# Scores of the next pair placed behind the output and state sums, with those sums in ring banks

## The chip, the cores and the metric

The kernel runs on one core of a Trainium2 chip. The metric is the device time of one execution in microseconds (us), the median of several runs. A profile of one execution gives a span (first to last instruction) that is a few us shorter than that time. The engines are called as in the profile: PE is TensorE (PEld its weight loads), DVE is VectorE, ACT is ScalarE, POOL is GpSimd, SP is SyncE, which only issues transfers here.

## What is computed

The reference is a state-space layer in chunks (4 batches, 8 heads, 768 positions, head dimension 32, state dimension 16) followed by a bilinear feed-forward over all 3072 tokens:

```python
for c in range(nc):                                   # chunks of 32 in the reference
    cum = np.cumsum(la, axis=-1)
    L = np.exp(cum[..., :, None] - cum[..., None, :]) * causal
    M = np.einsum('bhin,bhjn->bhij', Cc, Bc) * L      # "scores", masked
    y = M @ xc + (Cc @ state) * np.exp(cum)           # within the chunk, and from the state
    state = decay_full * state + sum_j(Bc x xc * decay_from_j)
x = y.transpose(0, 2, 1, 3).reshape(3072, 256)
out = ((x @ w_a) * (x @ w_b)) @ w_out                 # 256 -> 1536 -> 256
```

The result does not depend on the length of the chunks; the kernel takes 128.

## The kernel before, in words

**Pairs.** The work is cut into 12 pairs p: two batches of the four (index bt within a pair) times one block of 128 positions. Pairs 0 and 1 are block 0, pairs 2 and 3 block 1, and so on. A pair's state comes from pair p-2. The decay factors are folded into B and C when they are scaled, so that the scores need only a 0/1 mask.

**What is done for one pair.**

- `load` brings B, C and x in; `scale` multiplies them on POOL (`bm`, `cm`, `x16`; lines 231 and 237).
- `transposes` turns `bm` and `cm` on PE into the bank TT, which is a part of the tile SC0 (line 255); ACT copies them out three times (`bt` twice at line 262, `ct` at line 263).
- `scores` makes 32 small matmuls (tiles of 32 rows by 64 columns) into the four banks SC0 and SC1 (line 276). `mask(product(p, m))` multiplies one of the four banks by the causal mask into `t1` on DVE (line 309), in the prologue sometimes on POOL by way of ACT (lines 306 and 307).
- `pv` makes the output: four inter-chunk matmuls from the state (`sbd`, line 352; not for block 0), 32 small ones for the sums within the block (line 318), and 16 small ones for the state sums (`ds_mm`, line 335). Then ACT copies the output into `X2T` (line 364). In the kernel before, all of this lies in the two banks of SC1.
- `state` updates the state on DVE (lines 386 and 388), and POOL spreads it into `sbd` (line 392) and scales it for later (`gU`, line 399).
- `unit(p, k2)`, six for each pair, is one sixth of the feed-forward's first layer: four matmuls with w_a into `aps`, four with w_b into `bps` (line 417), a copy of `aps` to `asb` on ACT (line 426) and the product of `bps` and `asb` into `hk` on DVE (line 427). `go` makes whole units one after the other.
- `out_half(p, bt)` is the second layer for one batch: 12 matmuls into `ops` (line 434), a copy on ACT (line 449), a store.

**Banks.** `psf` is a pool of four accumulation banks with one tag. `aps`, `bps`, `ops` (and in the changed kernel `py0`, `py1`) each take one of them. A bank can be written again when the last reader of its old tile is done. The other four banks are SC0 and SC1.

**Order.** The schedule is manual: each engine gets its instructions in the order in which the program writes them, and semaphores are put where one engine needs another. After a prologue for pairs 0 to 2 the loop from p = 3 interleaves the scores of pair p, the six units of pair p-1, the two output halves of pair p-2, the output and state sums of pair p and the transposes of pair p+1:

```python
    for p in range(3, NP):
        scores(p)
        ...
        h = unit(p - 1, 0)
        mask(product(p, 0))
        h()
        ...
        out_half(p - 2, 0)
        go((p - 1, 3))
        pull(p); pv(p); state(p)
        transposes(p + 1)
        out_half(p - 2, 1)
        go((p - 1, 4), (p - 1, 5))
```

(shortened; the masks 1 to 3, unit 1 and unit 2 lie where the dots are.) After the loop come the units of pair 11 with the halves of pair 10 between them, and then the halves of pair 11.

Of the kernel before, what the change touches and what calls it, by code (L numbers as in the profile page):

```python
# [22 lines left out]
def kernel(  # L23
# [103 lines left out]
    def load(p, eng=None):  # L127
        tiles(p)
        return [load1(eng or nc.sync, p, w, bt) for w in range(3) for bt in range(2)]
# [115 lines left out]
    def scale(p):  # L245
        scale_bc(p, 1, nc.gpsimd)
        scale_bc(p, 0, nc.gpsimd)
        scale_x(p, nc.gpsimd)

    def transposes(p, ps=None):  # L250
        s = st[p]
        TB, TC = (TT[:, 0:256], TT[:, 256:512]) if ps is None else [t_.bitcast(f16)[:, 0:256] for t_ in ps]
        for T_, src in ((TB, s["bm"]), (TC, s["cm"])):
            for r in range(2):
                nc.tensor.transpose(  # L255
                    T_[:, r * 128 : (r + 1) * 128], src[:, r].rearrange("p h n -> p (h n)"), ident
                )
        BT = mid.tile([128, 2, 2, 2, 64], f16, name="bt", tag="bt")
        CT = mid.tile([128, 2, Q], f16, name="ct", tag="ct")
        for e in range(2):  # L260
            o_ = BT[:, e].rearrange("p r t i -> p (r t i)")
            nc.scalar.activation(out=o_, in_=TB, func=AF.Copy, scale=par[:, e : e + 1])  # L262
        (nc.scalar.copy if ps is None else nc.vector.tensor_copy)(
            CT.rearrange("p t (i r) -> p r (t i)", r=2), TC.rearrange("p (r c) -> p r c", r=2)
        )
        s["BT"], s["CT"] = BT, CT

    def scores(p):
        BT, CT = st[p]["BT"], st[p]["CT"]
        for e in range(2):  # L270
            for r in range(2):
                for m in range(4):
                    for bt in range(2):
                        rows = slice(32 * m, 32 * m + 32)
                        c0 = (e * 2 + r) * Q
                        nc.tensor.matmul(  # L276
                            SC[m][64 * bt : 64 * bt + 64, c0 : c0 + Q],
                            BT[rows, e, r, bt],
                            CT[rows, bt],
                            start=True,  # L280
                            stop=True,
                            skip_group_check=True,
                            tile_position=(32 * m, 64 * bt),
                        )
        st[p]["T1"] = mid.tile([128, H, 2, Q], f16, name="t1", tag="t1")

    def product(p, m):

        return (
            st[p]["T1"][:, 2 * m : 2 * m + 2].rearrange("p e r q -> p e (r q)"),  # L290
            SC[m].rearrange("p (e c) -> p e c", e=2),
        )
# [18 lines left out]
    def pv_u(p, u, py, first):  # L311
        s = st[p]
        for r in range(2):
            for g in range(4):
                for bt in range(2):
                    h = u * 4 + g
                    k = slice(64 * bt, 64 * bt + 64)
                    nc.tensor.matmul(  # L318
                        py[bt][32 * g : 32 * g + 32, u * Q : (u + 1) * Q],
                        s["X16"][k, h, r, :],  # L320
                        s["T1"][k, h, r, :],
                        start=(first and u == 0 and r == 0),
                        stop=(r == 1),
                        skip_group_check=True,
                        tile_position=(64 * bt, 32 * g),
                    )

    def ds_mm(p, c0):
        s = st[p]
        s["DS"] = [SC1[:, bt, c0 : c0 + 2 * D] for bt in range(2)]  # L330
        for r in range(2):
            for m in range(4):
                for bt in range(2):
                    k = slice(64 * bt, 64 * bt + 64)
                    nc.tensor.matmul(  # L335
                        s["DS"][bt][32 * m : 32 * m + 32, :],
                        s["bm"][k, r, 2 * m : 2 * m + 2, :].rearrange("p h n -> p (h n)"),
                        s["X16"][k, 2 * m : 2 * m + 2, r, :],
                        start=(r == 0),
                        stop=(r == 1),  # L340
                        skip_group_check=True,
                        tile_position=(64 * bt, 32 * m),
                    )

    def pv(p):
        blk, bp = divmod(p, NBP)
        s = st[p]
        PY = [SC1[:, bt, 0:256] for bt in range(2)]
        if blk > 0:
            for bt in range(2):  # L350
                for u in range(2):
                    nc.tensor.matmul(  # L352
                        PY[bt][:, u * Q : (u + 1) * Q],
                        s["Sbd"][:, bt, u * 128 : u * 128 + 128],
                        s["CT"][:, bt],
                        start=(u == 0),
                        stop=False,
                        skip_group_check=True,
                    )
        for u in range(2):  # L360
            pv_u(p, u, PY, blk == 0)
        if blk < NBLK - 1:
            ds_mm(p, 256)
        nc.scalar.activation(  # L364
            out=X2T[:, p].rearrange("p u t q -> p t u q"),
            in_=SC1[:, :, 0:256].rearrange("p t (u q) -> p t u q", u=2),
            func=AF.Copy,
            scale=YS / XS,
        )

    def evac0(u, bt, eng, py):
        o_, i_ = X2T[:, 0, u, bt], py[bt][:, u * Q : (u + 1) * Q]
# [34 lines left out]
    def unit(p, k2):  # L407
        s = st[p]
        if k2 == 0:
            s["hk"] = ffh.tile([128, NK, 2 * Q], f16, name="hk", tag="hk")  # L410
        a_ps = psf.tile([128, 512], f32, name="aps", tag="ff")
        b_ps = psf.tile([128, 512], f32, name="bps", tag="ff")
        for ps, W in ((a_ps, Wa), (b_ps, Wb)):
            for kk in range(2):
                k = 2 * k2 + kk
                for f in range(2):
                    nc.tensor.matmul(  # L417
                        ps[:, kk * 2 * Q : (kk + 1) * 2 * Q],
                        W[:, f, k * 128 : (k + 1) * 128],
                        X2T[:, p, f].rearrange("p t q -> p (t q)"),  # L420
                        start=(f == 0),
                        stop=(f == 1),
                        skip_group_check=True,
                    )
        asb = ffh.tile([128, 512], f32, name="asb", tag="asb")
        nc.scalar.copy(asb, a_ps)  # L426
        return lambda: nc.vector.tensor_tensor(  # L427
            out=s["hk"][:, 2 * k2 : 2 * k2 + 2, :].rearrange("p k q -> p (k q)"), in0=b_ps, in1=asb, op=ALU.mult
        )
# [23 lines left out]
    def out_half(p, bt):  # L453
        o_ps = psf.tile([128, 512], f32, name="ops", tag="ff")
        out_mm(p, bt, o_ps, range(NK))
        out_store(p, bt, o_ps)


    def bank(name):
        return psf.tile([128, 512], f32, name=name, tag="ff")  # L460

    def fb(k):
        nc.vector.reciprocal(flat(fB, k, k + 1), flat(fC, k, k + 1))  # L463

    def go(*items):
        for p, k2 in items:
            unit(p, k2)()

    def pull(p):
        if ("S", p) in st:  # L470
            st[p].update(st.pop(("S", p)))
# [68 lines left out]
    nc.scalar.copy(G.rearrange("p b g -> p (b g)"), gps[:, 0 : nb * NG])  # L540
    fb(1)
    scale(2)
    pv(1)
    ds_mm(0, 320)
    state(0)
    state(1)
    go((1, 0), (1, 1))
# [11 lines left out]
    h = unit(1, 4)  # L559
    mask(product(2, 1))  # L560
    h()
    go((1, 5))
    pull(2)
    pv(2)
    state(2)
    fb(2)
    load(4)
    transposes(3)
    out_half(0, 0)
    out_half(0, 1)  # L570

    for p in range(3, NP):
        scores(p)
        if p + 1 < NP:
            scale(p + 1)
        if p + 2 < NP:
            load(p + 2)
        h = unit(p - 1, 0)
        mask(product(p, 0))
        h()  # L580
        mask(product(p, 1))
        mask(product(p, 2))
        h = unit(p - 1, 1)
        h()
        mask(product(p, 3))
        go((p - 1, 2))
        out_half(p - 2, 0)
        go((p - 1, 3))
        pull(p)
        pv(p)  # L590
        state(p)
        if p + 1 < NP:
            transposes(p + 1)
        out_half(p - 2, 1)
        if p % 2 == 0 and p // 2 + 1 < NBLK:
            fb(p // 2 + 1)
        go((p - 1, 4), (p - 1, 5))

    go((NP - 1, 0), (NP - 1, 1))
    out_half(NP - 2, 0)  # L600
    go((NP - 1, 2), (NP - 1, 3))
    out_half(NP - 2, 1)
    go((NP - 1, 4), (NP - 1, 5))
    o = [psf.tile([128, 512], f32, name="ops", tag="ff") for _ in range(2)]
    for bt in range(2):
        out_mm(NP - 1, bt, o[bt], range(NK - 2))
# [33 lines left out]
```

## Time and profile before

| what | value | from |
|---|---|---|
| time, median of 3 runs | 137.73 us (137.08 to 137.8) | times |
| span of the profiled execution | 134.0 us | page |
| DVE line 427 (`hk`) | 72 x 687 ns | page, groups |
| ACT line 426 (`asb`) | 72 x 587 ns | page, groups |
| DVE line 309 (mask) | 44 x 681 ns | page, groups |
| ACT line 262 (`bt`) | 22 x 472 ns | page, groups |
| ACT line 449 (copy of an output half) | 23 x 385 ns | page, groups |
| POOL line 392 (`sbd`) | 10 x 1159 ns, 36.0 us idle before it | page, groups |
| ACT line 426 waits for PE's `aps` | 18.4 us, 45 times | waits |

How to read it: the page gives, for each engine, the busy time and its share of the span; below that the span in 40 equal slices with a digit for the busy tenths and one for the clock that PE was granted. A row of the groups names the line, the engine, the operation, the tiles written and read with their shapes, and the count; behind the bar stand the busy time, the mean duration of one, the idle time of the engine ahead of it and what ended that idle time. A row of the timeline has the start in us, the duration in us, the engine, the line, the operation, the tiles and the count; in brackets the idle time ahead of it and who ended it. Ends of matmuls are modelled, and neighbouring matmuls overlap in the record, so distances between starts are the better measure on PE.

### The profile page before, as it was taken

To read this page: it belongs to the slowest core of one execution; us is meant where nothing else is said; L and a number is where in the kernel's file an instruction comes from. 1 tells how busy PE (TensorE), PEld (TensorE's weight loads), DVE (VectorE), ACT (ScalarE), POOL (GpSimd) and SP (SyncE) were. 2 spreads that over 40 slices of the span, in tenths; PEclk is the share of its full clock that TensorE was granted. 3 is DMA by queue.
4 is the path that set the end of the run, shared out by engine and by line. 5 is a ranking of instruction groups with operands and counts; after the bars stand their busy time and mean duration, and the time that the engine had idled before them with its cause. 6 is when DMAs were issued, how large, how long until landed. Compare 5 with 4: busy or idle time off the path is not lost.

```text
span 134.0 us, 4722 instructions
## 1 busy us (share of the span) xinstructions
PE 125.1 (93%) x1946; PEld 102.8 (77%) x1946; DVE 86.2 (64%) x162; ACT 75.1 (56%) x154; POOL 55.5 (41%) x74
## 2 busy tenths in 40 slices
PE   6985798998999999999999999999999999999990
PEld 2332675887888888889888888888888888888870
DVE  1676138678277595793994974975947929834440
ACT  3162454696457647657548556576476576455420
POOL 6941906699940922904706608409128000000000
PEclk9999756999999999999999999999999999999999
DMA  3999999955146262451551451623611011110112
GB/s 72 169 179 195 159 188 178 183 102 112 42 86 151 72 117 64 91 109 39 108 134 39 64 137 54 111 80 72 126 47 39 5 50 33 39 39 5 41 37 78
DMA packets 44805, 12.22 MB, mean 91 GB/s; under 512 B 38576, under 2 KB 44752, under 8 KB 44784
## 3 DMA queue, kind: packets, MB, share of 16 engines
q1 hardware_dynamic: 38784, 9.04, 32.1%
q0 software_dynamic: 3216, 2.36, 12.2%
q10 hardware_dynamic: 2784, 0.52, 2.3%
q8 instruction: 15, 0.25, 0.8%
q14 instruction: 6, 0.05, 0.1%
HBM read 11.13 MB, written 3.15 MB: 107 GB/s over the span
## 4 chain that ended last, share of the span: by engine, by line
PE 73%; DMA 9%; SPq 8%; POOL 6%; issue 1%; DVE 0%; POOLq 0%
PE ops L434 24%; PE aps L417 20%; PE bps L417 20%; DMA xn<-in_x_dram 9%; SPq L122 8%; PE SC L276 2%; PE SC L318 2%; PE SC L255 2%; POOL sbd L392 2%; PE SC L352 1%; POOL t L307 1%; POOL x L231 1%; PE SC L335 1%; POOL gU L399 1%; POOL bm L237 0%
## 5 line engine op out<-in xcount | busy, mean ns | idle before, releaser
L427 DVE TENSOR_TENSOR hk<-bps,asb 128x512 f16<-128x512 f32 x72 | 49.3, 687 | 28.7 <-ACT asb L426 24.6
L426 ACT COPY asb<-aps 128x512 f32<-128x512 f32 x72 | 42.1, 587 | 20.0 <-PE aps L417 18.4
L417 PE MATMUL aps<-X2T,Wa 128*128 128x256 f16 x288 | 44.3, 277 | 0.0
L417 PE MATMUL bps<-X2T,Wb 128*128 128x256 f16 x288 | 44.2, 277 | 0.0
L434 PE MATMUL ops<-Wo,hk 128*128 128x256 f16 x288 | 35.0, 273 | 0.0
L417 PEld LDWEIGHTS <-Wb 128*128 128x128 f16 x288 | 28.5, 99 | 4.1 <-issue 0.2
L309 DVE TENSOR_TENSOR t<-SC,causal 128x512 f16<-128x512 f32 x44 | 29.0, 681 | 3.7 <-ACT osb L449 2.4
L417 PEld LDWEIGHTS <-Wa 128*128 128x128 f16 x288 | 27.4, 99 | 4.7 <-DVE X2T L376 0.3
L434 PEld LDWEIGHTS <-hk 128*128 128x128 f16 x288 | 27.7, 98 | 3.2
L392 POOL TENSOR_TENSOR sbd<-U,maskbd 128x512 f16<-128x512 f32 x10 | 11.6, 1159 | 36.1 <-DVE U L388 36.0
L449 ACT ACTIVATE osb<-ops 128x256 f32<-128x256 f32 x23 | 8.9, 385 | 17.0 <-PE ops L434 16.9
L231 POOL TENSOR_SCALAR x<-xn 128x512 f16<-128x512 f32 x10 | 14.9, 1492 | 1.9 <-DMA xn<-in_x_dram 1.1
L262 ACT ACTIVATE bt<-SC,ch 128x256 f16<-128x256 f16 x22 | 9.2, 472 | 2.7 <-PE SC L255 2.5
L364 ACT ACTIVATE X2T<-SC 128x512 f16<-128x512 f32 x11 | 6.6, 597 | 6.5 <-PE SC L335 4.8
L237 POOL TENSOR_TENSOR cm<-cn,fC 128x256 f16<-128x256 f32 x11 | 6.8, 621 | 3.1 <-DMA cn<-in_C_dram 3.1
L237 POOL TENSOR_TENSOR bm<-bn,fB 128x256 f16<-128x256 f32 x11 | 6.8, 622 | 0.9 <-DVE fB L463 0.9
L388 DVE SCALAR_TENSOR_TENSOR U<-SC,G,gU 128x64 f32<-128x64 f32 x16 | 3.8, 280 | 4.7 <-ACT X2T L364 4.7
L307 POOL TENSOR_TENSOR t<-tmp,causal 128x512 f16<-128x512 f32 x4 | 4.6, 1154 | 5.0 <-ACT tmp L306 5.0
L185 PE MATMUL SC<-warm 128*128 128x512 f16 x10 | 4.8, 628 | 1.2 <-DVE warm L149 1.2
L276 PE MATMUL SC<-ct,bt 32*64 32x128 f16 x384 | 5.9, 234 | 0.1
L276 PEld LDWEIGHTS <-bt 32*64 32x64 f16 x384 | 3.9, 109 | 2.7 <-issue 1.9
L255 PE MATMUL SC<-ident,bm 128*128 128x128 f16 x22 | 3.1, 224 | 2.6 <-POOL bm L237 2.6
(59 smaller groups left out, 73.2 us busy)
## 6 DMA issues: line engine op xcount, KB each, us to landing
xn<-in_x_dram SPq DMA_DIRECT2D x23, 128.0 KB, 3.1
out_dram<-osb SPq DMA_DIRECT2D x23, 128.0 KB, 1.7
bn<-in_B_dram SPq DMA_DIRECT2D x24, 64.0 KB, 2.7
cn<-in_C_dram SPq DMA_DIRECT2D x20, 64.0 KB, 3.1
Wa<-in_moe_w_a_dram POOLq DMA_DIRECT2D x3, 256.0 KB, 5.6
Wb<-in_moe_w_b_dram POOLq DMA_DIRECT2D x3, 256.0 KB, 6.5
Wo<-in_moe_w_out_dram POOLq DMA_DIRECT2D x1, 768.0 KB, 10.8
cn<-in_C_dram ACTq DMA_DIRECT2D x4, 64.0 KB, 4.6
```

The costliest lines, as they stand in the source:

```text
L122: return eng.dma_start(pair_in[p][which][64 * bt : 64 * bt + 64].rearrange("i h r n -> i h (r n)"), src.rearrange("h (i r) n -> i h (r n)" ...
L231: eng.tensor_scalar(xo, xi, XS, None, ALU.mult)
L237: eng.tensor_tensor(out=m_, in0=pair_in[p][which].rearrange("p h r n -> p r h n"), in1=f[:, blk, :, bp].unsqueeze(3).broadcast_to((128, 2, ...
L262: nc.scalar.activation(out=o_, in_=TB, func=AF.Copy, scale=par[:, e : e + 1])
L276: nc.tensor.matmul(SC[m][64 * bt : 64 * bt + 64, c0 : c0 + Q], BT[rows, e, r, bt], CT[rows, bt], start=True, stop=True, skip_group_check=True,
L309: nc.vector.tensor_tensor(out=o_, in0=i_, in1=c_, op=ALU.mult)
L392: nc.gpsimd.tensor_tensor(out=Sbd.rearrange("p t (m c) -> p t m c", m=4), in0=U32[:, p].unsqueeze(2).broadcast_to((128, 2, 4, 2 * D)), in1 ...
L417: nc.tensor.matmul(ps[:, kk * 2 * Q : (kk + 1) * 2 * Q], W[:, f, k * 128 : (k + 1) * 128], X2T[:, p, f].rearrange("p t q -> p (t q)"), sta ...
L426: nc.scalar.copy(asb, a_ps)
L427: return lambda: nc.vector.tensor_tensor(out=s["hk"][:, 2 * k2 : 2 * k2 + 2, :].rearrange("p k q -> p (k q)"), in0=b_ps, in1=asb, op=ALU.mult)
L434: nc.tensor.matmul(o_ps[:, 0:d_model], hk[:, k, bt * Q : (bt + 1) * Q], Wo[:, k, :], start=(k == 0), stop=(k == NK - 1), skip_group_check= ...
L449: nc.scalar.activation(out=o_sb, in_=o_ps[:, 0:d_model], func=AF.Copy, scale=1.0 / (YS * YS))
```

## The change

The tiled matmuls of the scores (32 x 64 tiles) and those of the output and state sums (64 x 32 tiles) stood at two places of a loop turn, with full-size feed-forward matmuls between them. The change puts the scores of pair p+1 directly behind the output and state sums of pair p, so that the small tiled matmuls come in one stretch. For this the output and state sums can no longer lie in SC1, which the scores write; they go into two banks of the ring (`py0`, `py1`). The rest of the turn follows from that: both output halves of pair p-1 come next, then the six units of the same pair p, with the transposes of pair p+2 between units 3 and 4. Scaling and loading run one pair further ahead. The masks of pair p+1 are issued in one go behind the first output half. The copy into `X2T` becomes one for each batch. In the prologue `transposes(3)` moves ahead of unit (1, 5), scores(3) behind `pv(2)`, and the halves of pair 1 come directly behind those of pair 0.

```diff
-    def ds_mm(p, c0):
+    def ds_mm(p, py, c0):
         s = st[p]
-        s["DS"] = [SC1[:, bt, c0 : c0 + 2 * D] for bt in range(2)]
+        s["DS"] = [py[bt][:, c0 : c0 + 2 * D] for bt in range(2)]
...
     def pv(p):
-        blk, bp = divmod(p, NBP)
-        s = st[p]
-        PY = [SC1[:, bt, 0:256] for bt in range(2)]
+        blk = p // NBP
+        py = [bank("py0"), bank("py1")]
         if blk > 0:
...
+            inter(p, py)
         for u in range(2):
-            pv_u(p, u, PY, blk == 0)
+            pv_u(p, u, py, blk == 0)
         if blk < NBLK - 1:
-            ds_mm(p, 256)
-        nc.scalar.activation(
-            out=X2T[:, p].rearrange("p u t q -> p t u q"),
-            in_=SC1[:, :, 0:256].rearrange("p t (u q) -> p t u q", u=2),
-            func=AF.Copy,
-            scale=YS / XS,
-        )
+            ds_mm(p, py, 256)
+        return py
+
+    def evac(p, py):
+        for bt in range(2):
+            nc.scalar.activation(
+                out=X2T[:, p, :, bt],
+                in_=py[bt][:, 0:256].rearrange("p (u q) -> p u q", u=2),
+                func=AF.Copy,
+                scale=YS / XS,
+            )
...
-    pv(1)
-    ds_mm(0, 320)
+    py = pv(1)
+    ds_mm(0, py, 320)
+    evac(1, py)
...
     h()
+    transposes(3)
     go((1, 5))
     pull(2)
-    pv(2)
+    py = pv(2)
+    scores(3)
+    evac(2, py)
     state(2)
     fb(2)
     load(4)
-    transposes(3)
     out_half(0, 0)
+    mask(product(3, 0))
     out_half(0, 1)
+    mask(product(3, 1))
+    scale(4)
+    load(5)
+    out_half(1, 0)
+    mask(product(3, 2))
+    out_half(1, 1)
+    mask(product(3, 3))
+    go((2, 0), (2, 1), (2, 2), (2, 3))
+    transposes(4)
+    go((2, 4), (2, 5))
 
     for p in range(3, NP):
...
+        pull(p)
+        py = pv(p)
         if p + 1 < NP:
-            scale(p + 1)
+            scores(p + 1)
+        evac(p, py)
+        state(p)
         if p + 2 < NP:
...
+            scale(p + 2)
+        if p + 3 < NP:
+            load(p + 3)
+        out_half(p - 1, 0)
         if p + 1 < NP:
...
+            for m in range(4):
+                mask(product(p + 1, m))
+        out_half(p - 1, 1)
+        go((p, 0), (p, 1))
+        if p % 2 == 1 and (p + 3) // 2 < NBLK:
+            fb((p + 3) // 2)
+        go((p, 2), (p, 3))
+        if p + 2 < NP:
+            transposes(p + 2)
+        go((p, 4), (p, 5))
```

More of the change, by code (lines that the diff above doesn't have):

```diff
@@ L343, in ds_mm, with inter @@
                     )
+    def inter(p, py):
+        s = st[p]
+        for bt in range(2):
+            for u in range(2):
+                nc.tensor.matmul(
+                    py[bt][:, u * Q : (u + 1) * Q],
+                    s["Sbd"][:, bt, u * 128 : u * 128 + 128],
+                    s["CT"][:, bt],
+                    start=(u == 0),
+                    stop=False,
+                    skip_group_check=True,
+                )
     def pv(p):
-        blk, bp = divmod(p, NBP)
-        s = st[p]
-        PY = [SC1[:, bt, 0:256] for bt in range(2)]
+        blk = p // NBP
+        py = [bank("py0"), bank("py1")]
         if blk > 0:
[L350 to L358, printed above, removed]
-                    )
+            inter(p, py)
         for u in range(2):
-            pv_u(p, u, PY, blk == 0)
+            pv_u(p, u, py, blk == 0)
         if blk < NBLK - 1:
-            ds_mm(p, 256)
-        nc.scalar.activation(
-            out=X2T[:, p].rearrange("p u t q -> p t u q"),
-            in_=SC1[:, :, 0:256].rearrange("p t (u q) -> p t u q", u=2),
-            func=AF.Copy,
-            scale=YS / XS,
-        )
+            ds_mm(p, py, 256)
+        return py
+    def evac(p, py):
+        for bt in range(2):
+            nc.scalar.activation(
[3 more added lines that the diff above has]
+                scale=YS / XS,
+            )
     def evac0(u, bt, eng, py):
@@ L567 @@
     load(4)
-    transposes(3)
     out_half(0, 0)
+    mask(product(3, 0))
     out_half(0, 1)
+    mask(product(3, 1))
[8 more added lines that the diff above has]
+    go((2, 4), (2, 5))
     for p in range(3, NP):
-        scores(p)
+        pull(p)
+        py = pv(p)
         if p + 1 < NP:
-            scale(p + 1)
+            scores(p + 1)
+        evac(p, py)
+        state(p)
         if p + 2 < NP:
[L577 to L591, printed above, removed]
-        if p + 1 < NP:
[L593 to L603, printed above, removed]
+            scale(p + 2)
+        if p + 3 < NP:
+            load(p + 3)
+        out_half(p - 1, 0)
+        if p + 1 < NP:
+            for m in range(4):
[8 more added lines that the diff above has]
+        go((p, 4), (p, 5))
     o = [psf.tile([128, 512], f32, name="ops", tag="ff") for _ in range(2)]
```

## The prediction

> **What bounds the kernel now.** I read the page's busy table and slices first, to see which engine could set the end; then the stages of the loop; then the timeline of TensorE over one pair; then the timelines of ScalarE and GpSimd at two places of the prologue.
>
> ```profile
> PE 125.1 (93%) x1946; PEld 102.8 (77%) x1946; DVE 86.2 (64%) x162; ACT 75.1 (56%) x154; POOL 55.5 (41%) x74
> ...
> PEclk9999756999999999999999999999999999999999
> ```
>
> TensorE is busy in 93% of the span and the granted clock is full but for three slices before 24 us. A busy share is an average, so the stages come next (columns: stretch, length, PE busy and count, clock, DMA share, GB/s):
>
> ```profile
> 54.65:64.03 9.38, 9.38 (x162) 1.00 0.40 86
> 64.03:73.42 9.39, 9.39 (x164) 1.00 0.40 86
> 73.42:82.80 9.38, 9.38 (x163) 1.00 0.40 87
> ```
>
> Each stretch is one turn of the main loop (from the scores of one pair to those of the next). It has no gap on TensorE. So a turn gets shorter only by TensorE work that goes away, and every wait that the change puts in front of TensorE is paid in full. The turn in start order (start, duration):
>
> ```profile
> 54.12 0.60 PE L417 MATMUL bps<-X2T,Wb 128*128 128x256 f16 x4
> 54.65 0.43 PE L276 MATMUL SC<-ct,bt 32*64 32x128 f16 x32
> 55.01 0.61 PE L417 MATMUL aps<-X2T,Wa 128*128 128x256 f16 x4
> 55.45 0.60 PE L417 MATMUL bps<-X2T,Wb 128*128 128x256 f16 x4
> ...
> 59.82 0.39 PE L352 MATMUL SC<-ct,sbd 128*128 128x128 f16 x4
> 60.14 0.42 PE L318 MATMUL SC<-t,x 64*32 64x128 f16 x32
> 60.39 0.32 PE L335 MATMUL SC<-x,bm 64*32 64x64 f16 x16
> 60.65 0.28 PE L255 MATMUL SC<-ident,bm 128*128 128x128 f16 x2
> 60.77 0.28 PE L255 MATMUL SC<-ident,cm 128*128 128x128 f16 x2
> 60.88 1.47 PE L434 MATMUL ops<-Wo,hk 128*128 128x256 f16 x12
> ```
>
> I use distances between starts, since a matmul's end is modelled. A group of four feed-forward matmuls takes 0.44 us (55.01 to 55.45), a unit of two groups 0.875, one output half 1.31 (60.88 to the next group at 62.19). Four 128-column matmuls take 0.23 in the transposes (60.65 to 60.88), but 0.32 where the tiled output sums follow (59.82 to 60.14), and a group takes 0.53 where the tiled scores follow (54.12 to 54.65). So **going between full and tiled matmuls costs about 0.1 us**. A turn is 6 units 5.25 + 2 halves 2.62 + 0.45 for the scores (0.09 before, 0.36 with the way back) + 1.06 for inter-chunk, output sums, state sums and transposes (59.82 to 60.88) = 9.38.
>
> **The Trainium skill.** "TensorEngine Tiling (Array Packing)", Key Properties, says that a change of tiling mode drains TensorE; the 0.09 to 0.1 us above agree. "PSUM — Partial Sum Buffer", Engine vs sequencer instructions, says that matmuls start and complete in program order; so one that waits for a bank holds all behind it, and the timeline shows no exception. "Perfetto Trace Analysis", Optimization Strategy, says that the same gap repeating on the engine that should be saturated can mean that there is too little SBUF or PSUM for the next tile. Before has no such gap in the loop; I expect after to get one.
>
> **Part 1: scores moved behind the state sums.** No matmul is added or removed. A turn before changes between full and tiled four times: into and out of the scores, and around the output and state sums. After, the tiled groups stand together: in, from state sums to scores (both tiled, other shapes), and out. If the change between two tiled shapes also costs 0.1, a turn saves one change, 0.1; if it is free, 0.2; if 16 small state sums run badly into the scores, 0. I take 0.1, keep 0 and 0.2. It acts on about 7 turns after the prologue: **-0.7 us** (0 to -1.4).
>
> **Part 2: the output sums move into the ring of four banks (psf).** Before, they lay in SC1, which nothing else needed then. Now py0 and py1 take two ring banks directly behind units 4 and 5. Which banks, the built program tells by its waits: py0 waits for ScalarE's copy of unit 4's aps, py1 for its copy of unit 5's aps (a bank is handed on in order of release). What ScalarE does just then: the transposes of pair p+2 now stand before units 4 and 5, so three copies of transposes (bt, bt, ct) stand in its queue ahead of those two copies. Before had 1.31 us of an output half between transposes and units. The prologue of before has exactly the new sequence once (transposes of pair 2, two units, then other work):
>
> ```profile
> 25.29 0.59 ACT L426 COPY asb<-aps 128x512 f32<-128x512 f32 x1 [0.29 <-PE aps L417]
> 25.89 0.84 ACT L262 ACTIVATE bt<-SC,ch 128x256 f16<-128x256 f16 x2
> 26.62 0.45 ACT L263 COPY ct<-SC 128x256 f16<-128x256 f16 x1
> 26.92 1.08 ACT L426 COPY asb<-aps 128x512 f32<-128x512 f32 x2
> ```
>
> There the transposes start at 25.47 and the last group of the second unit at 27.00, so TensorE is free at 27.44. The two copies end at about 27.5 and 28.00. Put py0 and py1 there: py0's two matmuls start at about 27.5 and take 0.11; py1 could start at 27.55 but waits for 28.00 and the way of the semaphore. For that way the trace gives 0.04 (L364 ends 23.48, ds_mm(0) starts 23.52) to 0.2. So **TensorE stands 0.5 us in every turn** (0.45 to 0.65). Behind the waiting py1 matmul stand output sums, state sums, next scores and both halves, so nothing fills it. A floor for the case that ScalarE is faster than I think: without transposes, aps 5 starts 0.875 before TensorE is free, the copy starts 0.69 after that (52.81 to 53.50), takes 0.59, ends at +0.40, and py1 would start at +0.11: still 0.35 with the semaphore. The turns into pairs 3 to 10 have transposes (8 x 0.5 = 4.0), the one into pair 11 has none (0.35). Sum **+4.35** (3.1 to 5.6). The py banks of pair 2 come free before the wait of Part 3, and cost nothing.
>
> **Part 3: the prologue.** transposes(3) moves ahead of unit (1,5) and pv(2). It needs bm of pair 3 from GpSimd:
>
> ```profile
> 29.25 2.28 POOL L307 TENSOR_TENSOR t<-tmp,causal 128x512 f16<-128x512 f32 x2
> 31.48 0.62 POOL L237 TENSOR_TENSOR cm<-cn,fC 128x256 f16<-128x256 f32 x1
> 32.06 0.62 POOL L237 TENSOR_TENSOR bm<-bn,fB 128x256 f16<-128x256 f32 x1
> ```
>
> GpSimd works without a gap from 24.71, when x of pair 2 lands, to 32.68, and its order up to there stays. TensorE before fills that time with unit (1,5) and pv(2) and waits 0.37. After, it comes to the transposes at 30.52 (where aps of unit (1,5) starts now) and waits until 32.73: 2.2 us. Laid out after: transposes 32.73, unit (1,5) 32.95, inter-chunk 33.83 (0.32), output sums (0.25), state sums (0.26), scores(3) 34.66 (0.36), four halves to 40.26, four units to 43.76, transposes(4), two units to 45.73, then 0.83 for pair 3's inter-chunk, output and state sums: scores(4) at 46.56 without Part 2's wait, against 45.26 before. **+1.3 us** (0.9 to 1.6). The halves of pairs 0 and 1, now all four together, are the same work.
>
> **What costs nothing.** The copy into X2T becomes two (about 0.38 each for 128x256, as L449, in place of 0.60): it ends under the first half. The masks of p+1 (4 x 0.68) follow the state update on VectorE and end about 0.4 before the first hk product is due, hidden by the two halves. bt and ct of p+1 come a turn ahead. GpSimd keeps its amount and has had 5 us idle a turn (L392). ds_mm(0) no longer waits for the X2T copy, but unit (1,0) then waits for the later copy; that lies ahead of Part 3's wait. The tail has the same units and halves without gap.
>
> Sum: 1.3 + 4.35 - 0.7 = +4.95; 137.73 + 4.95 = **142.7 us** (what lies outside the 134.0 us span is taken as unchanged).
>
> **Rivals.**
> A: the banks come free in time, and only the prologue and the saved change remain: 137.73 + 1.3 - 0.7 = 138.3. For it: ScalarE is 56% busy. Against: the wait hangs on the order of its queue, not on its load. Chance 0.08.
> B: faster. No bank wait, both changes of mode saved (-1.4), and the late transposes made up: 136.3. For it: the loop is TensorE alone, so a saved change counts in full. Against: 2.2 us in the prologue, where before hides work there. Chance 0.07.
> C: worse. Each wait is 0.9 rather than 0.5 since delays add up: the state update must leave py0 before aps of unit 0, and masks push the first hk products, which hold banks: 142.7 + 9 x 0.4 = 146.3. For it: four banks serve 16 tiles a turn in place of 14. Against: I count some 0.4 us of slack there. Chance 0.08.
> Forecast: 0.77.
>
> **How the numbers follow.** With the ends of its terms the forecast spans about 2.6 to 7.2 above before, but the ends will hardly meet; 140.2 to 144.6 holds it but for a little. Left out are A, B and most of C, 0.2. Slower by over 0.5% (above 138.4): the forecast, C and a part of A, 0.87; within: most of A, 0.06; faster: B, 0.07.
>
> **What would show it.** A gap of some 0.5 us on TensorE before or within the inter-chunk matmuls (line 352 before), released by ScalarE's asb copy (426), 8 or 9 times; a turn of about 9.8; a wait of about 2.2 us at the transposes at 30.5, released by GpSimd's bm; state sums to the next output half about 0.6 (0.26 and 0.36). It is wrong if the inter-chunk matmuls follow the units without a gap, if bm of pair 3 comes earlier, or if a new wait for VectorE appears ahead of unit 0.

## The result, and the profile after

The changed kernel takes 142.74 us (median of 4 runs, 141.11 to 142.92) against 137.45 us for the kernel before beside it: ratio 1.0324, 95% interval 1.0248 to 1.04. Times here and below are medians of all runs, while a ratio is formed from the fast runs alone and is not the quotient of the two medians; two kernels below have a single fast run and no ratio. The ratio stands for 4.5 us of 137.45, the medians differ by 5.3. Single executions of one kernel lie up to a few us apart, and in the traces they differ in the first 40 us (last section), while turns of the loop repeat to 0.01 us; the parts are therefore compared in the traces.

The page of the changed kernel, busy times and granted clock:

```profile
PE 126.1 (89%) x1946; PEld 103.9 (74%) x1946; DVE 87.1 (62%) x162; ACT 75.3 (53%) x165; POOL 55.4 (39%) x74
...
PEclk9999555999999999999999999999999999999999
```

TensorE runs the same 1946 matmuls (126.1 us busy, before 125.1) in 89% of the span where it was 93%: it has got gaps. The stages show where (one turn each, from the first output half of a turn to that of the next; length, then busy time and count of PE, PEld, DVE, ACT, POOL, clock, DMA share, GB/s):

```profile
59.66:69.44 9.78, 9.56 (x174) 8.27 (x161) 6.94 (x12) 5.88 (x14) 4.16 (x5) 1.00 0.34 72
69.44:79.22 9.78, 9.56 (x173) 8.27 (x161) 7.12 (x13) 5.88 (x14) 4.16 (x5) 1.00 0.43 94
79.22:88.99 9.77, 9.55 (x171) 8.25 (x161) 6.93 (x12) 5.88 (x14) 4.16 (x5) 1.00 0.38 82
```

A turn is 9.78, where it was 9.38 without any gap. The timeline of TensorE at the end of a turn (start, duration, idle time ahead and who ended it):

```profile
57.54 0.60 PE L424 MATMUL bps<-X2T,Wb 128*128 128x256 f16 x4
58.11 0.27 PE L349 MATMUL py<-ct,sbd 128*128 128x128 f16 x2
58.59 0.27 PE L349 MATMUL py<-ct,sbd 128*128 128x128 f16 x2 [0.21 <-ACT asb L433]
58.80 0.42 PE L318 MATMUL py<-t,x 64*32 64x128 f16 x32
59.05 0.32 PE L335 MATMUL py<-x,bm 64*32 64x64 f16 x16
59.30 0.43 PE L276 MATMUL SC<-ct,bt 32*64 32x128 f16 x32
59.66 2.79 PE L441 MATMUL ops<-Wo,hk 128*128 128x256 f16 x24
```

The group at 57.54 is free to be followed at 57.98 (0.44 a group). The two matmuls into py0 start at 58.11, 0.13 late, and the two into py1 at 58.59 instead of 58.22 (two of 0.055 behind py0's). Together 0.50 us in which TensorE stands. The bracket says only 0.21, since the ends of matmuls are modelled; the distances between starts give it whole. The chain of waits in the same stretch (start, length, what):

```profile
57.16 0.45 ACT ct L263
57.61 0.94 ACT asb L433 x2
58.55 0.04 issue
58.59 0.27 PE py L349 x2
```

It runs from the third copy of the transposes (`ct`) through the two `asb` copies, of units 4 and 5, to py1. The waits view counts 8 such places (total in us, times, longest; by modelled ends, so too small here as well):

```profile
PE py L349 <- ACT asb L433: 1.7, 8, 0.2
```

In the prologue, TensorE and GpSimd at transposes(3):

```profile
33.05 0.60 PE L424 MATMUL bps<-X2T,Wb 128*128 128x256 f16 x4
35.20 0.29 PE L255 MATMUL SC<-ident,bm 128*128 128x128 f16 x2 [1.55 <-POOL bm L237]
```

```profile
33.95 0.62 POOL L237 TENSOR_TENSOR cm<-cn,fC 128x256 f16<-128x256 f32 x1
34.52 0.62 POOL L237 TENSOR_TENSOR bm<-bn,fB 128x256 f16<-128x256 f32 x1
```

From 33.49 (33.05 and a group) to 35.20 TensorE stands 1.7 us until GpSimd's `bm` is there at 35.14.

**The sum in the traces.** From scores(4) to the end of the span: 88.7 before (45.26 to 134.0), 91.6 after (49.52 to 141.1), +2.9, which is 7 x (0.50 - 0.11) + 0.13. From scores(2) to scores(4): 17.73 before, 19.02 after, +1.29, of which 0.50 is the first bank wait, so 0.8 is the prologue's own. Together **+4.2 us**. The medians differ by 5.3. The two profiled executions differ by 7.1 (134.0 and 141.1), the other 2.9 of it ahead of scores(2) (27.53 before, 30.50 after), in code that the change hardly touches: the copies into X2T, and the state sums of pair 0 in the ring. But the profiled execution of before is a quick one: times are 1.7 above spans in every run with both (142.82 and 141.1), so by this estimate it took about 135.7, some 1.7 below its median. What is left for the start in the medians is then about 1 us.

### The profile page after: what moved, and what is told of

The parts are those of the page before. It is cut to its first block, busy times and chain, and to the rows that moved or that the text cites. A ratio compares the mean times of both kernels' runs of the same rounds, so it can differ in the third digit from the quotient of the medians.

```text
span 141.1 us, 4729 instructions
## 1 busy us (share of the span) xinstructions
PE 126.1 (89%) x1946; PEld 103.9 (74%) x1946; DVE 87.1 (62%) x162; ACT 75.3 (53%) x165; POOL 55.4 (39%) x74
## 4 chain that ended last, share of the span: by engine, by line
PE 70%; DMA 9%; ACT 9%; issue 5%; POOL 2%; ACTq 1%; DVE 0%; POOLq 0%
PE ops L441 23%; PE aps L424 17%; PE bps L424 17%; DMA cn<-in_C_dram 9%; ACT asb L433 5%; PE SC L276 3%; PE py L318 3%; ACT ct L263 3%; PE SC L255 2%; PE py L349 2%; PE fps L207 1%; PE py L335 1%; POOL cm L237 1%; POOL bm L237 1%; POOL t L307 1%
## 5 line engine op out<-in xcount | busy, mean ns | idle before, releaser
L433 ACT COPY asb<-aps 128x512 f32<-128x512 f32 x72 | 41.5, 593 | 13.3 <-PE aps L424 12.6
L441 PE MATMUL ops<-Wo,hk 128*128 128x256 f16 x288 | 33.3, 273 | 0.0
L424 PEld LDWEIGHTS <-Wa 128*128 128x128 f16 x288 | 28.0, 100 | 4.8 <-issue 1.0
L309 DVE TENSOR_TENSOR t<-SC,causal 128x512 f16<-128x512 f32 x44 | 27.4, 681 | 2.1 <-PE SC L276 2.1
L371 ACT ACTIVATE X2T<-py 128x256 f16<-128x256 f32 x22 | 7.3, 381 | 8.3 <-PE py L335 6.9
L255 PEld LDWEIGHTS <-bm 128*128 128x128 f16 x24 | 2.1, 99 | 7.7 <-POOL bm L237 6.3
L349 PE MATMUL py<-ct,sbd 128*128 128x128 f16 x40 | 5.3, 217 | 1.7 <-ACT asb L433 1.7
L395 DVE SCALAR_TENSOR_TENSOR U<-py,G,gU 128x64 f32<-128x64 f32 x16 | 4.0, 283 | 4.0 <-ACT X2T L371 3.3
L349 PEld LDWEIGHTS <-sbd 128*128 128x128 f16 x40 | 3.4, 96 | 4.0 <-issue 2.7
```

What stands on the lines that cost most here:

```text
L255: nc.tensor.transpose(T_[:, r * 128 : (r + 1) * 128], src[:, r].rearrange("p h n -> p (h n)"), ident)
L309: nc.vector.tensor_tensor(out=o_, in0=i_, in1=c_, op=ALU.mult)
L349: nc.tensor.matmul(py[bt][:, u * Q : (u + 1) * Q], s["Sbd"][:, bt, u * 128 : u * 128 + 128], s["CT"][:, bt], start=(u == 0), stop=False, s ...
L424: nc.tensor.matmul(ps[:, kk * 2 * Q : (kk + 1) * 2 * Q], W[:, f, k * 128 : (k + 1) * 128], X2T[:, p, f].rearrange("p t q -> p (t q)"), sta ...
L441: nc.tensor.matmul(o_ps[:, 0:d_model], hk[:, k, bt * Q : (bt + 1) * Q], Wo[:, k, :], start=(k == 0), stop=(k == NK - 1), skip_group_check= ...
```

## The experiments

Times are medians; the ratio is to the kernel before in the same set of runs (median 136.59 us for x1, x2, x3 and x5; 137.58 for x6, x7, w_before and w_after; 136.01 for w_after_again, x2w and x8), so times of different sets are not to be subtracted. "Turn" is the steady turn in the trace, "loop" the stretch from scores(4) to the end.

| kernel | turn | loop | time | ratio (95%) |
|---|---|---|---|---|
| before | 9.38 | 88.7 | 137.45 | 1 |
| changed | 9.78 | 91.6 | 142.74 | 1.0324 (1.0248 to 1.04) |
| x1_half_last | 9.69 | 91.1 | 141.55 | 1.0277 (1.0147 to 1.0407) |
| x2_transposes3_back | 9.77 | 91.6 | 142.01 | 1.0294 (1.0156 to 1.0432) |
| x3_ct_on_dve | 9.56 | 90.2 | 140.79 | 1.0297 (1.0203 to 1.0391) |
| x5_no_wait | 9.57 | 90.3 | 137.8 | none |
| x6_masks_spread | 9.28 | 88.0 | 136.62 | 1.0007 (0.9961 to 1.0054) |
| x7_ring_alone | 9.45 | 89.3 | 137.57 | none |
| w_before | 9.38 | 88.7 | 135.93 | 0.9916 (0.9855 to 0.9976) |
| w_after | 9.78 | 91.6 | 138.73 | 1.0214 (1.0157 to 1.0272) |
| w_after_again | 9.78 | 91.6 | 139.36 | 1.0185 (1.0108 to 1.0263) |
| x2w | 9.78 | 91.6 | 137.46 | 1.0118 (1.0051 to 1.0185) |
| x8_best | 9.28 | 88.0 | 133.26 | 0.9807 (0.974 to 0.9875) |

### x1_half_last: other work between the units and the sums

```diff
-        out_half(p - 1, 1)
         go((p, 0), (p, 1))
...
         go((p, 4), (p, 5))
+        out_half(p - 1, 1)
```

> The changed kernel with one move: the second output half of pair p-1 comes behind units 4 and 5 of pair p, so 1.31 us of work stands between the units and the next py0 and py1. Theory (the py matmuls wait for banks that ScalarE's copies of units 4 and 5 still hold): the gap of 0.5 us inside the inter-chunk matmuls goes away, the half itself waits some 0.1 for the copy of unit 4; a turn falls from 9.78 to about 9.4, the time by about 8 x 0.4 + 0.1 = 3.3 us, to about 139.4. Rival (the loss lies in the prologue and in the clock of TensorE before 25 us): the turn stays at 9.78 and the time at about 142.7.

Measured: the bank wait at the inter-chunk matmuls is gone, the half waits 0.13 for the copy of unit 4 (56.56 to 57.13, less a group of 0.44), as expected; but the turn is 9.69, not 9.4, and the time 141.55, not 139.4. TensorE in the new turn:

```profile
56.56 0.60 PE L424 MATMUL bps<-X2T,Wb 128*128 128x256 f16 x4
57.13 1.47 PE L441 MATMUL ops<-Wo,hk 128*128 128x256 f16 x12
58.43 0.39 PE L349 MATMUL py<-ct,sbd 128*128 128x128 f16 x4
58.75 0.42 PE L318 MATMUL py<-t,x 64*32 64x128 f16 x32
...
62.68 0.60 PE L424 MATMUL aps<-X2T,Wa 128*128 128x256 f16 x4
63.42 0.60 PE L424 MATMUL bps<-X2T,Wb 128*128 128x256 f16 x4
```

58.43 to 58.75 is the 0.32 that the inter-chunk matmuls took before. But a group of unit 2 now stands 0.74 ahead of the next one (62.68 to 63.42): a new gap of 0.30. So the theory of the bank wait holds and a second wait took most of the gain back. x5 and x6 show which.

### x2_transposes3_back and x2w: the prologue's part

```diff
-    transposes(3)
     go((1, 5))
     pull(2)
     py = pv(2)
-    scores(3)
...
     load(4)
+    transposes(3)
     out_half(0, 0)
     out_half(0, 1)
+    scores(3)
```

> The changed kernel with the prologue's transposes(3) back behind the sums of pair 2, and scores(3) behind the halves of pair 0; the loop is untouched. Theory: the wait of TensorE for GpSimd's bm of pair 3 (1.6 to 2.2 us at about 33.6) shrinks to about 0.3, two more changes of tiling mode cost 0.2; the time falls by about 1.3 us, to about 141.4; turns stay at 9.78. Rival (the wait only moves, since POOL sets the pace here and everything later follows it): unchanged, 142.7.

Measured: no wait at transposes(3); scores(2) to scores(4) takes 17.70 (after: 19.02), turns unchanged at 9.77. The time, 142.01, cannot be told from 142.74: in its trace TensorE ran at half clock for 13.7 us of the start, against 10.2. So it was repeated with a start that keeps the clock (see w_before):

> w_after with transposes(3) back behind the sums of pair 2. Theory: the wait of 1.55 for bm of pair 3 goes, two changes of mode cost 0.2, time 0.8 to 1.3 below w_after_again. Rival (in this stretch GpSimd's chain from the landing of x of pair 2 sets the pace, and the wait turns up at the next thing that GpSimd makes): less than 0.4 below.

Measured: 137.46, ratio 1.0118 (1.0051 to 1.0185), beside 139.36, ratio 1.0185 (1.0108 to 1.0263), without this edit: 0.0067 of 136, 0.9 us. GpSimd and TensorE of x2w at this place:

```profile
30.77 0.62 POOL L237 TENSOR_TENSOR bm<-bn,fB 128x256 f16<-128x256 f32 x1
```

```profile
31.72 0.28 PE L255 MATMUL SC<-ident,bm 128*128 128x128 f16 x2
```

`bm` is done at 31.39, before TensorE comes to the transposes. By the traces the rival, by which the wait only moves, falls: scores(2) to scores(4) takes 17.70 in both kernels with this edit, 1.32 less than the 19.02 of the changed kernel. The times alone do not show it, since the two intervals overlap. The 1.32 is more than the 0.8 that the prologue lost against before, because before had waits of its own there (0.37 for this `bm`).

### x3_ct_on_dve: is it the order of ScalarE's queue?

```diff
-        (nc.scalar.copy if ps is None else nc.vector.tensor_copy)(
+        (nc.scalar.copy if ps is None and p < 4 else nc.vector.tensor_copy)(
```

> The changed kernel with the third copy of the transposes (ct, 0.45 us) on VectorE in place of ScalarE for pairs 4 to 11. Theory (queue order on ScalarE delays the copies of units 4 and 5): these copies come 0.15 earlier until the copy of unit 5 meets its own floor of 0.35 us; the gap falls from 0.5 to 0.35 to 0.4, the time by about 1 us, to 141.7. Rival (the gap is the floor of a unit's own copy, whatever stands ahead of it): no change, 142.7.

Measured: a turn of 9.56, 0.22 less than 9.78, loop 90.2 against 91.6.

```profile
57.39 0.60 PE L424 MATMUL bps<-X2T,Wb 128*128 128x256 f16 x4
57.83 0.67 PE L349 MATMUL py<-ct,sbd 128*128 128x128 f16 x4
58.43 0.42 PE L318 MATMUL py<-t,x 64*32 64x128 f16 x32
```

py0 now follows without a gap (57.39 and 0.44), and from there to the output sums it takes 0.60 instead of 0.32: a gap of 0.28 is left. The two `asb` copies:

```profile
57.01 1.17 ACT L433 COPY asb<-aps 128x512 f32<-128x512 f32 x2
```

The second ends at 58.18. Half of 1.17 earlier, at about 57.60, it starts, 0.64 after the `aps` of unit 5 (56.96); where ScalarE is free, a copy starts 0.63 after its `aps` too (55.14 to 55.77 in the changed kernel). So the copy of unit 5 is no longer late, and the 0.28 is its floor; the other 0.22 of the 0.50 is the queue ahead of the copies. The rival, no change, falls by the turn, not by the time (ratio 1.0297 beside 1.0324, with overlapping intervals); the floor that I had put at 0.35 to 0.4 is too high.

### x5_no_wait and x6_masks_spread: what took its place

x5 puts everything together: the second half last, the transposes directly ahead of it, transposes(3) back.

```diff
...
         go((p, 4), (p, 5))
+        if p + 2 < NP:
+            transposes(p + 2)
+        out_half(p - 1, 1)
...
```

> All moves together: the second output half behind units 4 and 5, the transposes of pair p+2 directly ahead of that half (the order that the kernel before had), and transposes(3) back behind the sums of pair 2. Theory: no bank wait, no wait for bm; a turn of 9.28 (before: 9.38, less one change of tiling mode), time about 142.7 - 4.2 - 1.3 = 137.2, or some 0.5 below the kernel before if the start of the run is alike. Rival (the ring with 16 tiles a turn costs something wherever the sums stand): turns of 9.5 or more, time 139 or more.

Measured: turns of 9.57, time 137.8 (134.62 to 138.71). That is the rival's turn, but not by its reason: the inter-chunk matmuls have no wait, and the gap is once more at unit 2 (TensorE's timeline, then VectorE's, then the waits view):

```profile
55.57 0.60 PE L424 MATMUL aps<-X2T,Wa 128*128 128x256 f16 x4
56.30 0.60 PE L424 MATMUL bps<-X2T,Wb 128*128 128x256 f16 x4
```

```profile
53.18 2.47 DVE L309 TENSOR_TENSOR t<-SC,causal 128x512 f16<-128x512 f32 x4
55.57 1.28 DVE L434 TENSOR_TENSOR hk<-bps,asb 128x512 f16<-128x512 f32 x2
```

```profile
PE bps L424 <- DVE hk L434: 0.5, 1, 0.5
```

With one half in place of two ahead of the units, the four masks (53.18 to 55.65) still occupy VectorE when the first product `hk` is due; it ends about 56.26, and `bps` of unit 2 starts at 56.30 in the bank that it frees, 0.29 late (55.57 and a group are 56.01). The waits view names the releaser only once, in the turn from 90.42, where the gap is longer (93.85 to 94.93) and the modelled ends do not hide it. This is the second reason of the prediction's rival C, the masks: it does not act in the changed kernel, where two halves cover the masks, and it does where one is moved. x6 is x5 with one mask and the reciprocal (not in the cut shown) behind unit 5:

```diff
-            for m in range(4):
+            for m in range(3):
                 mask(product(p + 1, m))
...
         go((p, 4), (p, 5))
+        if p + 1 < NP:
+            mask(product(p + 1, 3))
```

> As x5 (second half behind the units, transposes directly ahead of it, transposes(3) back), and the fourth mask of pair p+1 and the reciprocal behind unit 5. In x5 a new gap of 0.29 stood before bps of unit 2. Theory (with one half only ahead of the units, the four masks still occupy VectorE when the first hk product is due, and bps of unit 2 waits for its bank): the gap goes away, a turn is 9.28, from scores(2) to the end some 2 us less than x5. Rival (bps of unit 2 waits for the state update or for ScalarE): the gap stays, 9.57.

```profile
57.85:67.13 9.28, 9.28 (x173) 8.23 (x161) 7.04 (x12) 6.13 (x14) 4.16 (x5) 1.00 0.41 88
67.13:76.41 9.28, 9.28 (x173) 8.23 (x161) 7.29 (x13) 6.13 (x14) 4.16 (x5) 1.00 0.41 87
76.41:85.68 9.27, 9.27 (x171) 8.21 (x160) 7.03 (x12) 6.12 (x14) 4.16 (x5) 1.00 0.40 87
```

Turns of 9.28 without a gap: 0.10 below the kernel before, which is what the scores behind the sums are worth. Loop 88.0, 0.7 below before. From scores(2) to the end it is 105.2 against 107.5 in x5, the 2 us expected, and against 106.5 in before. The times do not show this gain over before: the median is 0.96 lower (136.62 beside 137.58), but the ratio is 1.0007. The ring itself is not the cost: the same 16 tiles in four banks run here without a wait. Mask and reciprocal were moved together, so which of the two mattered is shown only by the timeline of x5 above.

### x7_ring_alone: the ring without the move

The kernel before, with `py0` and `py1` from the ring and `evac` for the one copy, and nothing else of the change.

> The kernel before with one part of the change alone: the output and state sums lie in two ring banks, with a copy for each bank; the order of the loop stays as before (an output half and one unit ahead of the sums). Theory (it is not the ring but its place directly behind two units and the transposes' copies that costs): a gap of at most 0.1 for the product of unit 2, turns of 9.38 to 9.5, time 0 to 1 us above the kernel before. Rival (16 tiles in four banks cost some 0.4 a turn wherever they stand): turns of 9.7 or more, time 3 to 4 us above.

Measured: turns of 9.45 (9.38 before), time 137.57 beside 137.58.

```profile
63.63 0.46 PE L349 MATMUL py<-ct,sbd 128*128 128x128 f16 x4
64.02 0.42 PE L318 MATMUL py<-t,x 64*32 64x128 f16 x32
```

0.39 in place of 0.32 at the inter-chunk matmuls: a wait of 0.07, by its place for a bank, and none elsewhere. So taking the sums into the ring costs next to nothing; taking them there directly behind two units and three copies costs 0.50.

### w_before, w_after, w_after_again and x8_best: the start taken out

```diff
     h()
+    warmup(8, SC[3])
     transposes(1)
```

> The kernel before, with 8 matmuls on zeros (128x512, some 0.21 us each) ahead of transposes(1), where TensorE stands 2.2 to 4.2 us waiting for B and C of pair 1. Theory (part of the difference between profiles is the start of a run: TensorE idle there, then a stretch of 6.8 to 10.2 us at half clock): the stretch at half clock gets shorter or goes away, the time falls by 1.7 to 3.4 us against the kernel before in most executions, and the spread shrinks. Rival (the half clock has nothing to do with this idle time): clock and time stay as they are.

> The changed kernel with the same 8 matmuls on zeros ahead of transposes(1). Theory: with a like start the change costs what its parts sum to from the second pair's scores on, 8 waits of 0.50 + 0.13 + 0.8 in the prologue - 7 x 0.11 = +4.2 us against the other kernel with these matmuls. Rival (the change also disturbs the start of the run): 5 us or more between the two.

> The changed kernel with the matmuls on zeros once more, on the chip of the next run. Both theories: as w_after, 138 to 139 and a loop of 91.6 from scores(4) to the end.

Measured: the matmuls on zeros bring 0.84% for the kernel before (135.93, ratio 0.9916 with 0.9855 to 0.9976), some 1.2 us and less than the 1.7 to 3.4 expected, and the changed kernel comes to 1.0214 and 1.0185. The two changed ones over the unchanged are 1.030 and 1.027, or 4.1 and 3.7 us on 137. With the intervals of the ratios that is some 3 to 5 us: it agrees with the 4.2 of the traces, and the times alone do not exclude 5.3 or the rival, a disturbed start. The loops are those of the kernels without the edit to 0.1 us. So the change costs some 4 us by the traces, and that the start of the executions added about 1 in the first comparison is the likely reading, not a shown one. In w_after_again the wait at transposes(3) was 3.7 us:

```profile
24.88 1.50 POOL L231 TENSOR_SCALAR x<-xn 128x512 f16<-128x512 f32 x1 [2.54 <-DMA xn<-in_x_dram]
32.89 0.28 PE L255 MATMUL SC<-ident,bm 128*128 128x128 f16 x2 [3.71 <-POOL bm L237]
```

There x of pair 2 landed late, at 24.88, and GpSimd stood 2.54 us for it; in w_after GpSimd started on it at 22.87 without a wait, and the wait at transposes(3) was 1.55. How long that wait is depends on when this transfer lands.

> x6 (no bank wait, turns of 9.28) with the 8 matmuls on zeros ahead of transposes(1). Theory: the loop from scores(4) to the end takes 88.0 (before 88.7), the start is that of w_before, so the time is some 2 us below the kernel before (w_before gained 0.8%, x6 0.0% with a wide spread). Rival (the start is bound by when x of pair 2 lands, and the matmuls on zeros only move the wait): no clear gain over x6.

Measured: 133.26 us, ratio 0.9807 (0.974 to 0.9875), the fastest of all: 2.6 us below the kernel before. Dividing by w_before gives 0.8% for the matmuls on zeros and 1.1% for the new order (0.9807 / 0.9916); that is an estimate across two sets. The traces give the new order 1.3 us (106.5 against 105.2 from scores(2) to the end), the ratio of x6, 1.0007, gives it nothing.

## Why the prediction was right

**Part 2, the banks, was right in mechanism and in size.** The eight waits are 0.50 each, and the turn is 9.78 where 9.38 - 0.1 + 0.5 was forecast. The sizes came from one place in the prologue of before that had the same sequence, and they carried over. The ninth wait, into pair 11, was put at 0.35 and is 0.13 (126.04 to 126.49 takes 0.45 instead of 0.32):

```profile
125.54 0.69 DVE L434 TENSOR_TENSOR hk<-bps,asb 128x512 f16<-128x512 f32 x1 [0.18 <-ACT asb L433]
125.80 0.59 ACT L433 COPY asb<-aps 128x512 f32<-128x512 f32 x1 [0.29 <-PE aps L424]
126.04 0.52 PE L349 MATMUL py<-ct,sbd 128*128 128x128 f16 x4
126.49 0.42 PE L318 MATMUL py<-t,x 64*32 64x128 f16 x32
```

The two matmuls into py1 start 0.21 before 126.49, at about 126.28: ahead of the end of ScalarE's copy of unit 5 (126.39), and 0.05 behind VectorE's product of unit 4 (126.23). So without transposes ahead, py1 takes the bank that this product frees, and the step "the turn into pair 11 has none (0.35)" took the handing-on of the other turns for granted. That term was mis-sized by 0.2.

**Part 1, the saved change of mode, was right.** It is 0.10 to 0.11 a turn: the sums follow one another in 0.25 (59.05 to 59.30) and the scores take 0.36, as forecast; x6 shows it as a whole, 9.28 against 9.38. A change between two tiled shapes was taken to cost what one to full matmuls costs. The runs agree with the sum, and no run separates the two.

**Part 3, the prologue, was right in mechanism and too large.** 1.3 (0.9 to 1.6) was forecast, and 0.8 is in the traces, below the range. The wait was put at 2.2 from the times of one execution of before; in the profiled execution after, GpSimd's chain stood nearer to TensorE's (scores(2) start to `bm` done: 4.64, in before 5.15), and the wait was 1.7 by starts. It is a difference of two chains which the start of the run shifts against each other (1.55 in w_after, 3.71 in w_after_again by the brackets), so one trace of before could not give it to 0.5 us.

**The rest.** That the forecast of 142.7 and the measured 142.74 agree to 0.1 us is luck: the forecast is +4.95 on 137.73, the traces give +4.2, and the medians +5.3 on 137.45, of which about 1 us is probably the start of the executions, of which the prediction said nothing. What it put at nothing stayed at nothing in the changed kernel: there is no wait for VectorE ahead of unit 0, the two copies into X2T end under the first half (0.66 in place of 0.60), and the tail is as before. Rivals A and B fall with the gap itself. Rival C did not act here, but one of its reasons, the masks, is real, as x5 shows.

## What to carry to other kernels

Where one engine fills the loop without a gap, ask of every moved tile whose buffer it takes and what the engine that frees that buffer has in its queue just then; 0.1 us saved a turn was paid with 0.5 because the next user of the ring stood directly behind its last two users. Putting independent work of the busy engine between the last tiles and the next taker, with the transposes, whose copies fill the other engine's queue, behind the units instead of ahead of them, and one mask later, brought the turn to 9.28, 0.1 below before. And when a piece of cover is moved, look at what else it covered: here the same output half hid the masks on VectorE.

## What the runs showed of the hardware

TensorE's clock in the start was not expected to differ from execution to execution. The clock records of the traces show stretches at half clock that are multiples of 3.41 us long: 6.83 in the profiled execution of before, 10.24 in that of after, 13.65 in x2_transposes3_back and x7_ring_alone, none in x5_no_wait. In the stages of before and of after (PE busy and count, clock, DMA share, GB/s):

```profile
15.34:22.16 6.82, 6.82 (x92) 0.50 1.19 171
```

```profile
14.62:24.82 10.20, 8.62 (x101) 0.50 1.01 148
```

Each belongs to the wait for B and C of pair 1: in before it begins 1.1 us behind 2.2 us of idle TensorE (12.02 to 14.23), in after, where B and C came 2 us later, within 4.2 us of it (12.00 to 16.20). With eight matmuls on zeros in that wait the stretch is absent in w_after, w_after_again, x2w and x8_best; w_before has one of 3.41 later, behind an idle time of 2.0 us for a mask of GpSimd's. The zeros are not free: in w_before `bm` of pair 1 was ready at 12.48, and the transposes started behind the zeros, at 13.62. The Trainium skill, "TensorE: Matmul & The Clock Gate", What's actually happening, says that the clock falls to half after an idle window of about 3.4 us, on a free-running window. The lengths agree with such a window. The idle time does not: 2.2 us in before was shorter than the page's window and was followed by half clock all the same, while x5_no_wait had the same 2.2 and kept its clock; why is open. By an estimate, 3.41 us at half clock cost up to 1.7 us of time, which is the size of the distance between the changed kernel's fastest run (141.11, mean clock 0.976) and its others (142.66 to 142.92, 0.962 to 0.964). But the clock is not the whole scatter: the profiled execution of w_after_again had full clock throughout and took 140.51, where others at full clock took 137.78 and 138.2. Its wait of 3.71 behind the late x of pair 2 is 2.2 longer than in w_after, the size of that distance.
